# Sliding-window attention with a gated feed-forward on one core: values 0 and 1 moved ahead of scores 2 and 3, and pairs of units scored by chunks of 64 keys

## The chip, the core and the metric

The kernel runs on one core of a Trainium2 chip. Times are device microseconds (us) of that core for one execution. Engines are named as in the profile: PE (TensorE, matrix products), PEld (its weight loads), DVE (VectorE), ACT (ScalarE), POOL (GpSimd) and SP (SyncE, which only issues DMAs here).

## What is computed

Attention of 8 batches, 8 heads, 576 positions and head size 64, in which each position sees those at most 32 away, and then two matrix products with a sigmoid gate between them:

```python
scores = scale * np.matmul(q, k.transpose(0, 1, 3, 2))
mask = np.abs(pos[:, None] - pos[None, :]) <= 32
attn = softmax(np.where(mask, scores, -1e9))
x = np.matmul(attn, v).transpose(0, 2, 1, 3).reshape(4608, 512)
h = x @ w_in                               # 512 x 2048
out = (h / (1 + np.exp(-1.702 * h))) @ w_out   # 2048 x 512
```

## The kernel before, in words

The 4608 rows of all batches are one long row of queries, shifted by 32, so that a block of 64 queries sees exactly two blocks of 64 keys. **A unit** is 128 queries (36 units, `NU`); **a tile** is four units, 512 rows (9 tiles, `NT`). Everything is issued by hand in one order (`tc.manual_schedule()`): each engine works through its own instructions in the order in which the program names them, and waits where a semaphore says so.

For a unit, `scores` (L274) writes into two PSUM banks, one for even and one for odd heads: for each of four head pairs and each parity three matmuls of 64x64 weights (the keys) over 64, 128 and 64 columns of queries. Keys 0 to 63 and the 64 keys of the next unit land on the lower 64 partitions, keys 64 to 127 on the upper. The parity picks the upper or lower 64 rows of the array. Two `Exp` activations on ACT (L290, 128x512 each) turn the two banks into p. `band` (L292) multiplies p by the mask on DVE, in place. `values` (L300) multiplies p with v on PE, 16 matmuls of 65 columns; the 65th column of v is 1 and gives the sum. Half of them take v itself (`ve`), half a copy shifted by 64 rows (`vo`), which POOL makes (`odd_v`, L213). `norm` (L318) divides on DVE: one reciprocal and one product where both halves stand in tag `t`, two of each where they stand in two single banks. `x_T` transposes x for the first product: on PE with a copy by the engine named, or by a DMA.

The feed-forward runs on PE between these. `layer1_plain` and `layer2_plain` are ordinary products; `l1_group` and `layer2` compute a 2x2 block product with 7 instead of 8 products, whose sums (`w1_sums`, `w2_sums`, `x_sums`, `g_sums`) are made on DVE.

PSUM has eight banks under tags: `t` (two banks) and the single banks `A`, `B`, `C`, `E`, `LA`, `LB`. A tag is free when its last reader is done. Tiles in SBUF come from rings: `p` had four buffers of one unit, `qT` seven of one unit.

The opening (L600 to L723) loads parts of k and q, then v 0 to 3 and part of v 4, then w_in in pieces of 256, 256, 512 and more columns. All these are DMAs on POOL's one queue; each issue waits for the landing of the eighth before it. In the opening there is no band for units 0 to 3: `seed` puts the mask as a bias into the banks ahead of the scores, one 128x512 matmul a bank. The order on PE before is: transposes of k, seed 0, transposes of q, seed 1, scores 0, scores 1, transposes of the rest of k and q, seeds 2 and 3, scores 2 and 3, values 0 and 1, transposes of x 0 and 1, values 2 and 3, the first product of w_in (`l1(0, 0)`), transposes of x 2 and 3, then products. They end with the k transposes of the next tile (L677, `T_four`), from where both kernels have the same order except in `scores`.

Later places that the change touches: scores 4 and 5 in the opening (L694, L695), scores 8 and 9 in `run` (L840, L841), and `front` (L755, L756, L762, L763), which scores four units ahead of each of the tiles 3 to 7. In `run`, `band(8)` and `band(9)` follow on DVE at once, and behind them are sums, norm 8, band 10 and norm 9.

Of the kernel before, what the change touches and what calls it, by code (L numbers as in the profile page):

```python
# [16 lines left out]
BF16 = mybir.dt.bfloat16  # L17
# [9 lines left out]
class _Kernel:  # L27
# [7 lines left out]
    def __init__(self, ctx, tc, q, k, v, w_in, w_out, out):  # L35
        self.tc, self.nc = tc, tc.nc
        self.q, self.k, self.v, self.w_in, self.w_out, self.out = q, k, v, w_in, w_out, out
        self.B, self.H, self.S, self.D = q.shape
        self.N = self.B * self.S
        self.DM = self.H * self.D  # L40
        self.DFF = w_in.shape[1]
        self.scale = 1.0 / (self.D ** 0.5)
        self.NU = self.N // 128
        self.NT = self.N // TILE

        def pool(name, bufs, **kw):
# [7 lines left out]
        self.g, self.gs, self.o, self.sc = {}, {}, {}, {}  # L54

# [99 lines left out]
    def kq_tile(self, t):  # L155

        if ("T", t) not in self.stage:
            s = self.sb("gs", [128, 4, 576 + TILE], BF16, 2, "kq4")
            k, q = self.stage["T", t] = s[:, :, 0:576], s[:, :, 576:]
            for i in range(4):  # L160
                self.kT[4 * t + i] = k[:, :, 128 * i:128 * i + 128]
                self.qT[4 * t + i] = q[:, :, 128 * i:128 * i + 128]
            self.kT[4 * t + 4] = k[:, :, 512:576]
        return self.stage["T", t]

    def T_first(self, c, part, tags, engs):
# [95 lines left out]
    def score_banks(self, tag):  # L262
        if tag == "t":
            sc = self.bank(tag, name="sc")
            return [sc[:, 0], sc[:, 1]]
        return [self.bank(x, name="sc") for x in tag]

    def seed(self, u, tag):

        self.sc[u] = self.score_banks(tag)  # L270
        for x in self.sc[u]:
            self.mm(x, self.ident, self.bias, start=True)

    def scores(self, u, tag=None):  # L274
        kT, q = self.kT[u], self.qT[u]
        nxt = self.k_first if u == self.NU - 1 else self.kT[u + 1][:, :, 0:64]
        bias = tag is None
        sc = self.sc.pop(u) if bias else self.score_banks(tag)
        for hp in range(4):
            c = 128 * hp  # L280
            start = hp == 0 and not bias
            for eo in range(2):
                r = slice(64 * eo, 64 * eo + 64)
                lo, hi = sc[eo][0:64], sc[eo][64:128]
                self.mm(lo[:, c:c + 64], kT[r, hp, 0:64], q[r, hp, 0:64], start=start)
                self.mm(hi[:, c:c + 128], kT[r, hp, 64:128], q[r, hp, :], start=start)
                self.mm(lo[:, c + 64:c + 128], nxt[r, hp, :], q[r, hp, 64:128], start=False)
        p = self.p[u] = self.sb("p", [128, 2, 8, SQ], BF16, 4)
        for eo in range(2):
            self.nc.scalar.activation(p[:, eo].rearrange("k h s -> k (h s)"), sc[eo], AF.Exp, scale=self.scale)  # L290

    def band(self, u, eng=None):  # L292
        p = self.p[u]
        cross = [(2 * u + i) % 9 == 8 for i in range(2)]
        a, b = 0 if cross[0] else 1, 2 if cross[1] else 3
        pv = p.rearrange("p e (h b) s -> p (e h) b s", b=2)
        msk = self.mask[:, a:b + 1:b - a, :].rearrange("p (o b) s -> p o b s", o=1)
        (eng or self.nc.vector).tensor_mul(pv, pv, msk.to_broadcast([128, 8, 2, SQ]))  # L298

    def values(self, u, tag):  # L300
# [10 lines left out]
        for h in range(self.H):  # L311
            o = slice((h % 4) * (D + 1), (h % 4 + 1) * (D + 1))
            for blk in range(2):
                vt = (self.ve[u % 9], self.vo[u % 5])[blk]
                self.mm(acc[h // 4][64 * blk:64 * blk + 64, o], p[:, h % 2, h // 2 * 2 + blk, :], vt[:, h, :D + 1],
                        start=(h % 4 == 0))

    def norm(self, u):  # L318
# [281 lines left out]
    def opening(self):  # L600
# [57 lines left out]
        def l1(half, *fs, **kw):  # L658
            for f in fs:
# [1 line left out]
                n[0] += 1  # L661

        l1(0, 0)
        self.x_T(2, "B", act)
        self.x_T(3, "E", dve)
        l1(0, 2)
        l1(1, 0, 2)
        dve.tensor_copy(self.k_first, self.kT[0][:, :, 0:64])
        dve.tensor_copy(self.v_first, self.ve[0][0:64])
        l1(0, 4, 6)  # L670
        l1(1, 4, 6)
        for i in (3, 1, 2, 4):
            self.w1_sums((i,), 0)
# [17 lines left out]
        for u in (8, 9, 10, 11):  # L691
            self.fetch(u)
        h[:], n[0] = ["LB", "LA"], 0
        self.scores(4, "AC")  # L694
        self.scores(5, "t")  # L695
        l1(None, 12, later=gelus, kept=kept[2])
        self.scores(6, "BE")
        self.band(4)
# [40 lines left out]
    def front(self, t, late):  # L739
# [12 lines left out]
            return  # L752
        self.l2eng = self.nc.vector
        u = 4 * t + 4
        self.scores(u, "t")  # L755
        self.scores(u + 1, "AC")  # L756
        do(late, 2)
        do(l2, 20)
        do(late)
        xs = self.x_sums(t)  # L760
        do(xs, 1)
        self.scores(u + 2, "BE")  # L762
        self.scores(u + 3, "t")  # L763
        do(l2, 12)
        do(xs)

# [63 lines left out]
    def run(self):  # L830
# [130 lines left out]
```

## Time and profile before

| | |
|---|---|
| median of 3 runs | 282.11 us (281.75 to 282.63) |
| the profiled execution | 282.34 us |
| its span, first to last instruction | 280.5 us |
| mean granted PE clock | 0.993 |
| busy: PE, PEld, DVE, ACT, POOL | 268.9, 222.7, 212.1, 195.5, 133.1 us |
| moved by DMA | 37.61 MB |

The profile is of one execution. Its times count from the first instruction; about 1.8 us of the execution lie outside the span. A row of a timeline is: start, length, engine, line of the program, operation, what it writes and reads, shape, count, and in brackets the idle time of the engine before it and what ended it. A row of the chain is: start, length, what the end of the program was waiting for in that stretch. Busy time of PE includes the time that a matmul's last columns take to come through the array, so back-to-back matmuls overlap in it.

### The profile page before, as it was taken

How to read it: one execution, taken by the hardware profiler on the slowest of the kernel's cores; microseconds unless marked ns; L12 is line 12 of the kernel's file. 1: busy time of each engine (PE TensorE's matmuls, PEld its weight loads, DVE VectorE, ACT ScalarE, POOL GpSimd, SP SyncE). 2: the span in 40 equal slices, each digit the busy share in tenths (PEclk: the TensorE clock that was granted, in tenths of full speed). 3: DMA queues.
4: the chain of work that ended last, by engine and by line, in shares of the span. 5: the costliest groups of instructions: out<-in, count | busy, mean ns of one | idle time of the engine just before them, and what ended most of it. 6: DMA issues, size and time to landing. Idle time of an engine off the chain costs nothing.

```text
span 280.5 us, 8889 instructions
## 1 busy us (share of the span) xinstructions
PE 268.9 (96%) x3648; PEld 222.7 (79%) x3648; DVE 212.1 (76%) x492; ACT 195.5 (70%) x343; POOL 133.1 (47%) x199
## 2 busy tenths in 40 slices
PE   1979999999999999999999999999999999999995
PEld 1558756776888888888888888888888888888884
DVE  4454698897987798788888797888788887945731
ACT  2576893889897689658875887687759775567411
POOL 8895695999498248745694619441210000000000
PEclk9979999999999999999999999999999999999999
DMA  8999999999999999999999999999922051201033
GB/s 87 167 204 198 179 207 164 192 135 148 116 162 149 185 157 169 127 219 119 193 150 201 136 166 96 215 146 150 166 56 84 2 115 21 75 2 75 2 112 116
DMA packets 150265, 37.61 MB, mean 134 GB/s; under 512 B 138064, under 2 KB 145872, under 8 KB 150224
## 3 DMA queue, kind: packets, MB, share of 16 engines
q0 software_dynamic: 106656, 18.42, 95.0%
q1 hardware_dynamic: 43120, 18.10, 36.5%
q8 instruction: 28, 0.46, 0.7%
q10 hardware_dynamic: 448, 0.52, 0.6%
q14 instruction: 13, 0.11, 0.1%
HBM read 36.83 MB, written 9.44 MB: 165 GB/s over the span
## 4 chain that ended last, share of the span: by engine, by line
PE 93%; DVE 2%; ACT 2%; issue 1%; POOL 1%; ACTq 0%; POOLq 0%; DVEq 0%
PE o L70 40%; PE h L70 40%; PE sc L70 5%; PE pv L70 5%; PE tp L177 1%; PE tp L244 1%; ACT kq L67 1%; POOL kq L152 1%; PE tp L344 1%; DVE x L328 1%; PE tp L356 0%; ACT L680 0%; PE tp L201 0%; DVE kq L67 0%; DVE mask L111 0%
## 5 line engine op out<-in xcount | busy, mean ns | idle before, releaser
L459 ACT ACTIVATE g<-h 128x512 f16<-128x512 f32 x128 | 72.2, 598 | 35.1 <-PE h L70 34.9
L222 POOL COPY vo<-ve 64x264 int32<-64x264 int32 x71 | 32.9, 463 | 63.6 <-PE pv L70 41.3
L70 PEld LDWEIGHTS <-g 128*128 128x128 f16 x576 | 54.5, 98 | 10.1
L70 PE MATMUL h<-xs,a 128*128 128x256 f16 x384 | 57.6, 272 | 0.0
L70 PEld LDWEIGHTS <-a 128*128 128x128 f16 x512 | 49.5, 98 | 9.3 <-DVE xs L388 0.2
L70 PE MATMUL o<-w,g 128*128 128x256 f16 (+1 forms) x320 | 55.0, 294 | 0.0
L70 PE MATMUL h<-xT,w 128*128 128x256 f16 (+1 forms) x368 | 54.4, 281 | 0.0
L70 PEld LDWEIGHTS <-w 128*128 128x128 f16 x496 | 48.0, 98 | 7.7
L70 PEld LDWEIGHTS <-gs 128*128 128x128 f16 x384 | 36.7, 98 | 4.9 <-issue 0.2
L290 ACT ACTIVATE p<-sc 128x512 bf16<-128x512 f32 x72 | 36.9, 616 | 3.1 <-PE sc L70 2.9
L70 PE MATMUL o<-b,g 128*128 128x256 f16 x256 | 38.3, 273 | 0.0
L70 PE MATMUL o<-b,gs 128*128 128x256 f16 x256 | 37.7, 273 | 0.0
L472 DVE TENSOR_TENSOR h<-h,s 128x512 f32<-128x512 f32 x32 | 22.3, 698 | 19.2 <-PE h L70 19.0
L211 POOL DMA_DIRECT2D ve<-in_v_dram x40 | 34.3, 864 | 5.2 <-DMA w<-in_moe_w_out_dram 2.1
L67 ACT COPY h<-h 128x512 f32<-128x512 f32 x32 | 18.8, 588 | 16.7 <-PE h L70 16.3
L328 DVE TENSOR_TENSOR x<-pv,rec 128x256 f16<-128x256 f32 (+1 forms) x52 | 27.4, 527 | 1.8
L141 POOL DMA_DIRECT2D qst<-in_q_dram x35 | 28.1, 809 | 0.3
L141 POOL DMA_DIRECT2D kst<-in_k_dram x31 | 26.5, 856 | 1.3 <-DMA w<-in_moe_w_out_dram 1.3
L478 DVE TENSOR_TENSOR h<-h,s 128x512 f32<-128x512 f32 x32 | 22.4, 699 | 6.2 <-PE h L70 5.9
L298 DVE TENSOR_TENSOR p<-p,mask 128x1024 bf16<-128x1024 bf16 x32 | 22.3, 698 | 0.1
L67 ACT COPY s<-h 128x512 f32<-128x512 f32 x32 | 19.2, 600 | 1.2
L70 PE MATMUL h<-xs,w 128*128 128x256 f16 x128 | 19.2, 273 | 0.0
(87 smaller groups left out, 340.6 us busy)
## 6 DMA issues: line engine op xcount, KB each, us to landing
out_dram<-o_sb SPq DMA_DIRECT2D x33, 256.0 KB, 4.1
ve<-in_v_dram POOLq DMA_DIRECT2D x32, 128.0 KB, 6.6
kst<-in_k_dram POOLq DMA_DIRECT2D x25, 128.0 KB, 6.3
qst<-in_q_dram POOLq DMA_DIRECT2D x21, 128.0 KB, 5.8
w<-in_moe_w_out_dram POOLq DMA_DIRECT2D x4, 512.0 KB, 11.2
w<-in_moe_w_in_dram POOLq DMA_DIRECT2D x3, 512.0 KB, 9.6
qst<-in_q_dram POOLq DMA_DIRECT2D x7, 96.0 KB, 4.6
kq<-in_q_dram POOLq DMA_DIRECT2D x2, 256.0 KB, 5.9
```

The lines of the kernel that those rows point to most:

```text
L67: (eng.copy if eng is self.nc.scalar else eng.tensor_copy)(out, in_)
L70: self.nc.tensor.matmul(out, lhsT, rhs, start=start, stop=stop, skip_group_check=True)
L141: self.nc.gpsimd.dma_start(t[off:off + n], src[b, :, s:s + n, :].rearrange("h s d -> s h d"))
L152: self.nc.gpsimd.dma_start(self.stage["first"][0:n // j, :, at:at + j], src[0, :, lo:lo + n, :].rearrange("h (p j) d -> p h j d", j=j))
L211: self.nc.gpsimd.dma_start(t[off:off + n, :, :self.D], self.v[b, :, s:s + n, :].rearrange("h s d -> s h d"))
L222: eng.tensor_copy(*((words(vo[64:128]), words(self.ve[u % 9][64:128])), (words(vo[0:64]), words(nxt)))[i])
L290: self.nc.scalar.activation(p[:, eo].rearrange("k h s -> k (h s)"), sc[eo], AF.Exp, scale=self.scale)
L298: (eng or self.nc.vector).tensor_mul(pv, pv, msk.to_broadcast([128, 8, 2, SQ]))
L328: dve.tensor_mul(x[:, 4 * at:4 * (at + n), :].rearrange("p (b h) d -> p b h d", b=n), acc[:, :, :, :D], r.to_broadcast([128, n, 4, D]))
L459: act.activation(g[:, f, 256 * half:256 * half + 256], bank.rearrange("p (i n) -> p i n", i=2), AF.Gelu_apprx_sigmoid)
L472: dve.tensor_add(e, b, s7)
L478: dve.tensor_add(c, b, s7)
```

## The change

- `scores_pair` scores two units at once. The 256 queries of a pair lie side by side in one tile (`qTT`, three buffers), and the keys are taken in five chunks of 64 which see 64, 128, 128, 128 and 64 queries. This makes 40 matmuls for what were 48, over the same 4096 columns. Bank order changes: the first two banks hold head pairs 0 and 1 of both units, the last two head pairs 2 and 3. It is used for units 0, 2, 4, 8 and in `front` for 4t+4 and 4t+6; units 6, 7 and 10 to 15 keep `scores`.
- The p of two units is one tile (two buffers in place of four). An `Exp` covers two head pairs of both units. Each unit's p is then eight runs of 128 elements, 256 apart.
- In the opening, values 0 and norm 0 stand ahead of seeds 2 and 3 and their scores; the second half of pair 2's exps (`late=True`) comes behind the copy of x 0 on ACT; `l1(0, 0)` stands ahead of values 2 and 3; the banks of several steps change.
- `load_w1(0, 256)` is issued ahead of `load_v(3)`.

```diff
@@ place
+        if c == "q":
+            if u % 2 == 0:
+                two = self.qTT[u] = self.sb("qTT", [128, 4, 256], BF16, 3)
+                for i in range(2):
+                    self.qT[u + i] = two[:, :, 128 * i:128 * i + 128]
+            return self.qT[u]
@@ seed
-        self.sc[u] = self.score_banks(tag)
-        for x in self.sc[u]:
+        for x in self.score_banks(tag):
+            self.sc.setdefault(u, []).append(x)
             self.mm(x, self.ident, self.bias, start=True)
@@ scores
-        p = self.p[u] = self.sb("p", [128, 2, 8, SQ], BF16, 4)
+        if u % 2 == 0:
+            self.pp = self.sb("p", [128, 2, 2, 8, SQ], BF16, 2)
+        p = self.p[u] = self.pp[:, u % 2]
@@ new
+    def scores_pair(self, u, tags=None, late=False):
+        k = [self.kT[u], self.kT[u + 1], self.k_first if u + 2 == self.NU else self.kT[u + 2]]
+        q = self.qTT.pop(u)
+        sc = [x for tag in tags for x in self.score_banks(tag)] if tags else self.sc.pop(u)
+        for hp in range(4):
+            c, start = 256 * (hp % 2), hp % 2 == 0 and tags is not None
+            for eo in range(2):
+                r = slice(64 * eo, 64 * eo + 64)
+                bank = sc[2 * (hp // 2) + eo]
+                for i in range(5):
+                    lo, hi = max(0, 64 * (i - 1)), min(256, 64 * (i + 1))
+                    rows = slice(64 * (i % 2), 64 * (i % 2) + 64)
+                    self.mm(bank[rows, c + lo:c + hi], k[i // 2][r, hp, rows], q[r, hp, lo:hi], start=start and i < 2)
+        p = self.sb("p", [128, 2, 2, 2, 4, SQ], BF16, 2)
+        for i in range(2):
+            self.p[u + i] = p[:, :, :, :, 2 * i:2 * i + 2, :]
+        def exps(x):
+            for eo in range(2):
+                self.nc.scalar.activation(p[:, eo, x].rearrange("k h b s -> k (h b s)"), sc[2 * x + eo], AF.Exp,
+                                          scale=self.scale)
+        exps(0)
+        if not late:
+            exps(1)
+        return lambda: exps(1)
@@ opening
-        for u in (0, 1, 2, 3):
+        for u in (0, 1, 2):
             self.load_v(u)
+        self.load_w1(0, 256)
+        self.load_v(3)
         self.load_v(4, slice(0, 1))
-        self.load_w1(0, 256)
...
-        self.seed(1, "AC")
-        self.scores(0)
-        self.scores(1)
+        self.seed(0, "AC")
+        self.scores_pair(0)
         self.T_first("k", 1, ("LA", "LB"), (dve, dve))
         self.T_first("q", 1, ("B", "E"), (dve, act))
-        self.seed(2, ("LA", "LB"))
-        self.seed(3, "AC")
-        self.scores(2)
-        self.scores(3)
         self.values(0, "t")
         self.norm(0)
-        self.values(1, ("B", "E"))
+        self.seed(2, ("LA", "LB"))
+        self.seed(2, ("B", "E"))
+        exps = self.scores_pair(2, late=True)
+        self.values(1, "AC")
         self.norm(1)
-        self.x_T(0, "LA", act)
-        self.x_T(1, "LB", act)
-        self.values(2, "t")
-        self.norm(2)
-        self.values(3, "AC")
-        self.norm(3)
-        h, n = ["LA", "LB", "A", "C", "B", "E"], [0]
+        self.x_T(0, "t", act)
+        exps()
+        self.x_T(1, "A", dve)
+        h, n = ["LA", "LB", "C", "A", "B", "E"], [0]
...
         l1(0, 0)
-        self.x_T(2, "B", act)
-        self.x_T(3, "E", dve)
+        self.values(2, "t")
+        self.norm(2)
+        self.values(3, "BE")
+        self.norm(3)
         l1(0, 2)
+        self.x_T(2, "t", act)
+        self.x_T(3, "B", dve)
+        l1(0, 4, 6)
         l1(1, 0, 2)
...
-        l1(0, 4, 6)
@@ opening, run and front: each two calls of scores(u, ..), scores(u + 1, ..) become one, as here
-        self.scores(8, "t")
-        self.scores(9, "AC")
+        self.scores_pair(8, ("t", "AC"))
```

More of the change, by code (lines that the diff above doesn't have):

```diff
@@ L163, in kq_tile @@
             self.kT[4 * t + 4] = k[:, :, 512:576]
+            for i in (0, 2):
+                self.qTT[4 * t + i] = q[:, :, 128 * i:128 * i + 256]
         return self.stage["T", t]
@@ L256, in seed, with scores @@
     def seed(self, u, tag):
-        self.sc[u] = self.score_banks(tag)
-        for x in self.sc[u]:
+        for x in self.score_banks(tag):
+            self.sc.setdefault(u, []).append(x)
             self.mm(x, self.ident, self.bias, start=True)
[L262 to L274, printed above, removed]
+    def scores(self, u, tag):
         kT, q = self.kT[u], self.qT[u]
         nxt = self.k_first if u == self.NU - 1 else self.kT[u + 1][:, :, 0:64]
-        bias = tag is None
-        sc = self.sc.pop(u) if bias else self.score_banks(tag)
+        sc = self.score_banks(tag)
         for hp in range(4):
             c = 128 * hp
-            start = hp == 0 and not bias
+            start = hp == 0
             for eo in range(2):
@@ L295, in band @@
         a, b = 0 if cross[0] else 1, 2 if cross[1] else 3
-        pv = p.rearrange("p e (h b) s -> p (e h) b s", b=2)
+        pv = (p.rearrange("p e (h b) s -> p (e h) b s", b=2) if len(p.shape) == 4 else
+              p.rearrange("p e y z b s -> p (e y z) b s"))
         msk = self.mask[:, a:b + 1:b - a, :].rearrange("p (o b) s -> p o b s", o=1)
@@ L314, in values @@
                 vt = (self.ve[u % 9], self.vo[u % 5])[blk]
[L315 removed]
+                w = p[:, h % 2, h // 2 * 2 + blk, :] if len(p.shape) == 4 else p[:, h % 2, h // 4, h // 2 % 2, blk, :]
+                self.mm(acc[h // 4][64 * blk:64 * blk + 64, o], w, vt[:, h, :D + 1],
                         start=(h % 4 == 0))
@@ L693, in opening @@
         h[:], n[0] = ["LB", "LA"], 0
-        self.scores(4, "AC")
-        self.scores(5, "t")
+        self.scores_pair(4, ("AC", "t"))
         l1(None, 12, later=gelus, kept=kept[2])
@@ L754, in front @@
         u = 4 * t + 4
-        self.scores(u, "t")
-        self.scores(u + 1, "AC")
+        self.scores_pair(u, ("t", "AC"))
         do(late, 2)
@@ L761, in front @@
         do(xs, 1)
-        self.scores(u + 2, "BE")
-        self.scores(u + 3, "t")
+        self.scores_pair(u + 2, ("BE", "t"))
         do(l2, 12)
```

2 lines of the change are left out of this document (1 added, 1 removed).

## The prediction

> **What bounds the kernel now.** I read the page first (span, clock line, chain by engine), then the chain and the timelines of the opening, then each place where the new pairs stand.
>
> ```profile
> span 280.5 us, 8889 instructions
> ...
> PE 93%; DVE 2%; ACT 2%; issue 1%; POOL 1%; ACTq 0%; POOLq 0%; DVEq 0%
> ```
>
> TensorE carries 93% of the chain that ended last, and from about 21 us on it hardly waits. So the change can win in two ways: fill the holes of the first 21 us, or make the score matmuls shorter. It loses wherever a new wait reaches TensorE. The page's clock line dips in the opening; three windows show it:
>
> ```profile
> 10.26:13.67 3.41, 3.07 (x103) 2.09 (x106) 1.89 (x3) 2.54 (x5) 2.56 (x6) 1.00 2.40 155
> 13.67:17.08 3.41, 2.05 (x87) 1.44 (x77) 1.93 (x6) 2.65 (x5) 3.15 (x7) 1.00 1.44 200
> 17.08:20.49 3.41, 3.24 (x45) 2.48 (x45) 1.93 (x6) 1.97 (x3) 3.41 (x5) 0.50 1.24 207
> ```
>
> The columns are window, length, busy us of PE, PEld, DVE, ACT and POOL, then the granted clock (1.00, 1.00, then 0.50) and the DMA. After a window with PE busy for 2.05 of 3.41 us the clock was halved for 3.4 us. The chain there:
>
> ```profile
> 16.20 0.43 DVE x L328
> ...
> 16.91 0.34 issue
> ...
> 17.51 1.02 PE pv L70 x16
> 18.53 1.82 PE h L70 x8
> 20.35 0.58 PE tp L344 x8
> 20.93 6.99 PE h L70 x64
> 27.91 1.06 PE tp L201 x32
> ```
>
> TensorE waits for VectorE's norm of unit 1, transposes, runs values 2 and 3, then at half clock the first 8 products with w_in (1.82 us; 64 of them at full clock take 6.99, so 8 take 0.87). The k transposes of the next tile (27.91) are my finish line for the opening: what stands in between is the same work in both kernels.
>
> **Part 1, the opening.** The rows that set the new order:
>
> ```profile
> 10.80 2.07 ACT L290 ACTIVATE p<-sc 128x512 bf16<-128x512 f32 x4 [0.70 <-PE sc L70]
> 12.73 1.33 POOL L222 COPY vo<-ve 64x264 int32<-64x264 int32 x3 [0.51 <-DVE kq L67]
> 12.74 0.81 PE L70 MATMUL sc<-bias,ident 128*128 128x512 bf16 x3 [0.22 <-DVE kq L67]
> 14.59 0.21 DVE L327 RECIPROCAL rec<-pv 128x8 f32<-128x8 f32 x1 [1.31 <-PE pv L70]
> 15.44 0.17 DVE L327 RECIPROCAL rec<-pv 128x4 f32<-128x4 f32 x1
> ```
>
> Values 0 now stand right behind the transposes of q. They need the four exps of pair 0 (10.80 + 2.07 = 12.87) and the first shifted copy of v, GpSimd's first of three from 12.73 (done about 13.14). So they start at 13.2; before, the norm's reciprocal of their result stood at 14.59, so they ran some 0.9 later. The four seeds of units 2 and 3 queue behind them, and behind those the pair's scores. Values take about 0.25 a unit, the four seeds 0.2 each, the pair's scores 0.5, each change of shape about 0.1; values 1 start near 15.1 and end at 15.4.
>
> VectorE gets norm 0 at 13.7, long before it matters, and norm 1 at 15.5. Norm 1 took from 15.44 to 16.63 before, so it ends near 16.65 now: later by the scores of the second pair that went ahead. What is late next is this norm; the transpose of x 1 ends near 17.0, its copy (0.42 on VectorE) near 17.5, and the first w_in product starts near 17.6 instead of 18.53. ScalarE runs exps(0), the copy of x 0, then the late exps: 15.0 + 1.0 + 0.5 + 1.1 = 17.6, before values 2 ask for them. Values 2 follow at 18.5, values 3 to 19.0, a product to 20.0, x 2 to 20.2. Norm 3 follows norm 2 on VectorE and ends near 21.0, so the transpose of x 3 ends at 21.2. Seven groups of 8 products are then left, 56 x 0.109 = 6.1: the k transposes start near 27.47 against 27.91. **Gain 0.44 us**, if the clock stays full from 13 us on.
>
> The w_in columns. Before, values 3, the rest of values 4 and both quarter loads of w_in were the DMAs that stood between values 2 and the 512-column load; they are exchanged, no byte is added. The first product doesn't start before 17.6 by the norms above, and the first quarter would have landed by 16.9 where it stood (issued at 9.30, 7.6 to landing):
>
> ```profile
> 9.30 2.41 POOL L125 DMA_DIRECT2D w<-in_moe_w_in_dram  x3
> w<-in_moe_w_in_dram POOLq DMA_DIRECT2D x1, 256.0 KB, 7.6
> 16.64 0.89 POOL L190 DMA_DIRECT2D o_sb<-in_k_dram  x1
> o_sb<-in_k_dram POOLq DMA_DIRECT2D x1, 512.0 KB, 9.3
> ```
>
> So it gains nothing. It makes GpSimd's copies of values 3 wait longer by one quarter load (256 KB at the window's 200 GB/s, 1.3 us), and what is queued behind them is the issue of the next k and q loads (16.64, now about 17.4). The k load takes 9.3 us to landing because it queues behind loads of w_in, so I cost this at nothing too; without that cover it is 0.8 us on a load that TensorE needs at 27.9.
>
> Ends for the opening: at best the half clock cost and the 0.34 issue gap are both gone and the norms overlap better, -0.9; at worst the half clock strikes a denser stretch, +0.6.
>
> **Part 2, 40 matmuls for 48.** Fourteen pairs: 0, 2, 4, 8, and 16 to 34. Columns streamed are the same.
>
> ```profile
> 128.75 0.70 PE L70 MATMUL sc<-qT,kT 64*64 64x64 bf16 x48
> 69.63 0.38 PE sc L70 x16
> 128.82 0.63 PE sc L70 x32
> L70 PE MATMUL sc<-qT,kT 64*64 64x128 bf16 x2 | 0.2, 240 | 0.0
> L70 PE MATMUL sc<-qT,kT 64*64 64x64 bf16 x2 | 0.2, 213 | 0.0
> ```
>
> The second and third rows are of the chain (some matmuls are merged there): one unit costs 0.38, two cost 0.63, so a further unit is 0.25. A unit puts eight 64-column matmuls on each of the two tiles of the array that hold keys 0 to 63; 0.25/8 = 31 ns each. The other two tiles have four of 128 columns, about 55 ns each by the 0.109 of a 256-column one. The last two rows are the first 35 ns of a batch: two of each shape have started, though the program's order is 64, 128, 64, 64, 128, 64. The second 128 passed the third 64, so the tiles run side by side and the fullest tile sets the time. In a pair it has 64, 128, 64 for each of four head pairs: 4 x (31 + 55 + 31) = 0.47, against 16 x 31 = 0.50. **0.03 us a pair.** Ends: 0, and eight matmuls at 0.63/48 = 13 ns, 0.10 us, if issue is what bounds. I take 0.02, nearest to the tiles' row, as the first pair of each front also waits for its bank C to come free: ten pairs in the fronts give **-0.2 us** (0 to -1.0).
>
> **Part 3, bands wait for four exps instead of two.** Each exp now covers two head pairs of both units, so band u needs the whole pair. In the steady fronts the bands run 2 us after the exps and feel nothing. At unit 8 they follow at once:
>
> ```profile
> 68.68 2.06 ACT L290 ACTIVATE p<-sc 128x512 bf16<-128x512 f32 x4
> 69.84 1.63 DVE L298 TENSOR_TENSOR p<-p,mask 128x1024 bf16<-128x1024 bf16 x2
> 71.39 0.42 DVE L402 TENSOR_TENSOR gs<-gs,g 128x512 f16<-128x512 f16 x1
> ...
> 74.51 0.42 DVE L328 TENSOR_TENSOR x<-pv,rec 128x256 f16<-128x256 f32 x1
> 74.99 0.22 PE L70 MATMUL pv<-ve,p 128*64 128x65 bf16 x1
> ```
>
> Band 8 began at 69.84, after two exps; now after four, at 68.68 + 2.06 = 70.74 and the 0.03 of a wake-up. Band 9 waited for the same fourth exp, and the g sum came 0.61 behind its start (71.39 - 70.78); with both bands behind that exp the g sum starts at 72.0, **0.61 late**, and the timeline shows no idle time of VectorE from there to 77 us that could make it good. Queued behind band 8 are band 9, two g sums, norm 8, band 10 and norm 9. Values 10 wait for norm 9 already: their second half started at 74.99, right after 74.51 + 0.42 = 74.93. So TensorE is held by nearly the whole delay: **+0.6 us** (0.4 to 0.6). At unit 4 the same, smaller:
>
> ```profile
> 33.54 4.05 ACT L290 ACTIVATE p<-sc 128x512 bf16<-128x512 f32 x8 [0.57 <-PE sc L70]
> 35.34 0.69 DVE L298 TENSOR_TENSOR p<-p,mask 128x1024 bf16<-128x1024 bf16 x1
> ...
> 38.12 0.68 DVE L298 TENSOR_TENSOR p<-p,mask 128x1024 bf16<-128x1024 bf16 x1
> 38.86 0.22 PE L70 MATMUL pv<-ve,p 128*64 128x65 bf16 x1
> ```
>
> The fourth exp ends at 33.54 + 2.07 = 35.61; band 4 moves from 35.34 to 35.64, and with what is queued behind it on VectorE (a copy, band 5, norm 4; a short idle time there gives 0.12 back) band 6 from 38.12 to 38.30, and values 6, which started 0.06 after band 6 ended, by **+0.18**. The band over a strided p keeps the same runs of 128 elements; I leave it at 0.69, and a dearer one would show first at unit 8. The transposed q written into half of a pair's tile and the two p tiles per pair have covers of tens of us.
>
> **Sum.** -0.44 - 0.2 + 0.6 + 0.18 = +0.15 us. The profiled execution took 282.34 us (span 280.5 and 1.8 around it), 0.23 above the median of 282.11. 282.34 + 0.15 = **282.5**: no change that a measurement tells.
>
> **Rivals.** (a) *The clock is halved again.* In the new order TensorE still waits from about 15.7 to 17.5, with short transposes between; windows of 3.41 us there hold, by the terms of part 1 and the 0.2 us that a lone matmul's busy time outlasts its stream, 2.3 us of busy PE (an estimate), a little over the 2.05 after which the clock was halved, well under the 3.07 of the window ahead of it, which kept it. If it strikes, the denser stretch pays: 8 products 0.9 us more, values 0.3, less what the norms cover, about 0.9: 283.4, slower. It decides from the point where 2.3 us of 3.41 count as too little. The Trainium skill ("TensorE: Matmul & The Clock Gate", Part 1) says that the clock falls after an idle window of some 3.4 us whose phase runs free. This trace agrees on the length (3.41 us at 0.50), while its window was 60% busy; by that page's idleness neither order would be throttled.
>
> (b) *Matmuls start strictly in order.* Then in a pair each head pair's second parity waits until the first's fifth matmul has started, 31 + 55 = 86 ns, twice per head pair: 4 x 172 = 0.69 us against 0.50, +0.19 for each pair, and 12 pairs on the path make +2.3, and the fronts' 0.2 is not won: 285.0. The Trainium skill (the same page, Part 3, what overlaps) has matmuls start in program order and only weight loads pulled ahead; the rows of the first 35 ns above speak against that here.
>
> (c) *Issue bounds the scores:* -0.10 a pair, 281.6. For it: 13 ns each fits 0.63/48; against it: 0.38 for 24 doesn't halve. (d) *The bands' delay is absorbed:* 281.7; against it stands the back-to-back VectorE from 69.84 to 77.
>
> **Chances.** Forecast 0.42, (a) 0.30, (b) 0.06, (c) 0.10, (d) 0.07, others 0.05. Within 0.3% (0.85 us, about what a measurement of this kernel tells from no change) are 0.33 of the forecast, 0.07 of (a), 0.06 of (c), 0.04 of (d): 0.50 in all. Slower are 0.08 of the forecast, 0.23 of (a), all of (b) and 0.02 of the others: 0.39. The rest, 0.11, is faster. The range takes in the forecast with its bounds, (a), (c) and (d), and leaves out (b): 281.2 to 284.0.
>
> **What would show it.** Right: the first w_in product near 17.6, the k transposes near 27.5; a pair of scores at 0.60 in the chain; band 8 starting at the end of the fourth exp and a hole of TensorE in values 10. Wrong: a clock of 0.50 between 17 and 22 us (then a); pairs at 0.5 (c) or 0.8 (b); no hole at unit 10 (d).

## The result, and the profile after

The changed kernel takes 283.93 us in the median of 21 runs (283.13 to 286.16), the kernel before 282.71 in 21 runs beside them. The ratio is 1.0049, with a 95% interval of 1.0032 to 1.0065: slower by about 1.4 us. The forecast was no change that a measurement tells (282.5); 283.93 lies inside its range of 281.2 to 284.0, but other terms make it up. The profiled execution of after took 283.94, so it is a typical one. Its page:

```profile
span 282.2 us, 8654 instructions
...
PEclk9999999999999999999999999999999999999999
...
PE 82%; ACT 5%; DMA 5%; DVE 4%; POOL 2%; issue 1%; POOLq 0%; DVEq 0%
```

No dip of the clock; but DMA, absent from the chain before, now holds 5% of it, and TensorE lost 11 points. The chain of after in the opening (start, length, what):

```profile
17.52 1.03 PE h L70 x8
18.55 0.39 PE pv L70 x16
...
21.06 0.28 PE tp L371 x2
21.34 6.11 PE h L70 x56
27.46 1.06 PE tp L203 x32
```

The first w_in product starts at 17.52 (forecast 17.6), the k transposes at 27.46 (forecast 27.47; 27.91 before). Unit 4 and unit 8 in the same chain:

```profile
33.08 2.07 ACT p L309 x4
35.16 0.02 issue
35.18 0.69 DVE p L324
...
68.95 1.58 ACT p L309 x3
70.53 0.02 issue
70.56 1.29 DVE p L324 x2
71.85 0.35 DVE gs L429
...
74.95 0.43 DVE x L355
75.39 0.04 issue
75.43 0.32 PE pv L70 x8
75.75 0.38 PE sc L70 x16
```

The bands start at the end of the fourth exp, both times, and at unit 8 VectorE then runs without a pause until values 10 get their bank. The scores of unit 13 start 0.44 after those of before (75.31), although TensorE was 0.25 ahead at 68.6. That was forecast; what follows was not:

```profile
100.07 0.51 issue
100.59 6.73 DMA xT<-x
107.32 0.03 issue
107.35 0.02 DVEq L415
107.37 0.04 issue
107.41 0.42 DVE xs L415
...
109.04 1.05 PE h L70 x8
```

Tile 3's sums of x wait for the DMA that transposes unit 15's x: issued at 100.59, landed at 107.32. TensorE loses 0.9 there. Another loss stands behind the last matmul. The rows of SyncE's last instructions (line of the kernel's end, engine's queue, operation, count: shortest, median, longest ns, first and last start), after and before:

```profile
L979 SPq DRAIN  x3: 7/7/122, 281.2 to 281.6; - x3
```

```profile
L956 SPq DRAIN  x3: 7/7/7, 279.7 to 280.0; - x3
```

The first drain comes 0.6 after the last store landed (280.60) instead of 0.27 (279.42), and takes 122 ns.

To see where each execution loses or gains, the start of the same matmul was compared in all traces. The table gives it in us against the first profiled execution of before; minus is earlier. Its places: first transpose of the next tile's k; the last matmuls of values 6; a layer 2 product ahead of unit 8's bands; values 11; a layer 2 product ahead of tile 3; a product behind the start of tile 5; the last tile. The k column is the first transpose's own start; the chain above counts its stretch 0.07 later. The last column is the time from the last matmul's end to the end of the span.

| trace | k (27.85) | values 6 (38.86) | 68.60 | values 11 (77.04) | 101.74 | 164.63 | 259.72 | end |
|---|---|---|---|---|---|---|---|---|
| before | 0 | 0 | 0 | 0 | 0 | 0 | 0 | 3.38 |
| before, again (e13) | -0.70 | -0.70 | -0.71 | -0.71 | -0.71 | -0.34 | -0.33 | 3.46 |
| after | -0.46 | -0.22 | -0.25 | +0.44 | +0.41 | +1.45 | +1.40 | 3.82 |
| after, again (e9) | -0.20 | +0.16 | +0.26 | +0.95 | +1.09 | +1.02 | +0.97 | 3.74 |
| e1 | -0.42 | -0.07 | -0.07 | -0.07 | -0.02 | -0.06 | -0.11 | 3.73 |
| e2 | -0.54 | -0.54 | -0.53 | -0.53 | -0.57 | -0.43 | -0.48 | 3.81 |
| e4 | -0.60 | -0.36 | -0.39 | +0.30 | +0.27 | +0.11 | +0.05 | 3.94 |
| e6 | -0.67 | -0.44 | -0.47 | +0.22 | +0.18 | +0.66 | +0.67 | 3.42 |
| e7 | -0.34 | +0.10 | +0.21 | +0.21 | +0.17 | +2.08 | +2.03 | 3.79 |
| e16 | -0.52 | -0.52 | -0.54 | -0.54 | -0.55 | +2.46 | +2.53 | 3.41 |

One more difference lies behind the last place. Before's chain has VectorE idle for 0.40 ahead of a copy in the last tile, for which no view names a reason:

```profile
275.25 0.40 issue
275.65 0.44 DVE o_sb L558
```

TensorE waits for that copy. The copy is VectorE's instruction 575 in the trace (its first has number 0), and the same delay of 0.40 to 0.41 stands ahead of number 575 in e13 and e4, where it is the same copy, and in e5, where it is the copy before. In the other 16 traces another instruction has that number, and TensorE's last eight products stand 0.21 earlier against before than the products ahead of them. So after's last matmul ends only 1.19 later than before's, not 1.40.

### The profile page after: what moved, and what is told of

The parts are those of the page before. It is cut to its first block, busy times and chain, and to the rows that moved or that the text cites. A ratio compares the mean times of both kernels' runs of the same rounds, so it can differ in the third digit from the quotient of the medians.

```text
span 282.2 us, 8654 instructions
## 1 busy us (share of the span) xinstructions
PE 269.3 (95%) x3536; PEld 221.9 (79%) x3536; DVE 212.9 (75%) x493; ACT 194.9 (69%) x342; POOL 132.3 (47%) x199
## 4 chain that ended last, share of the span: by engine, by line
PE 82%; ACT 5%; DMA 5%; DVE 4%; POOL 2%; issue 1%; POOLq 0%; DVEq 0%
PE h L70 37%; PE o L70 37%; PE pv L70 4%; PE sc L70 3%; DMA xT<-x 2%; DMA ve<-in_v_dram 2%; ACT p L309 2%; DVE p L324 1%; DVE x L355 1%; POOL kq L152 1%; PE tp L252 1%; ACT kq L67 1%; ACT g L486 1%; PE tp L383 0%; ACT L309 0%
## 5 line engine op out<-in xcount | busy, mean ns | idle before, releaser
L224 POOL COPY vo<-ve 64x264 int32<-64x264 int32 x71 | 32.1, 452 | 67.2 <-PE pv L70 44.8
L70 PE MATMUL h<-xT,w 128*128 128x256 f16 (+1 forms) x368 | 53.7, 277 | 0.6 <-ACT p L309 0.6
L309 ACT ACTIVATE p<-sc 128x512 bf16<-128x512 f32 x56 | 28.5, 621 | 2.9 <-PE sc L70 2.8
```

The costliest lines, as they stand in the source:

```text
L70: self.nc.tensor.matmul(out, lhsT, rhs, start=start, stop=stop, skip_group_check=True)
L224: eng.tensor_copy(*((words(vo[64:128]), words(self.ve[u % 9][64:128])), (words(vo[0:64]), words(nxt)))[i])
L309: self.nc.scalar.activation(p[:, eo, x].rearrange("k h b s -> k (h b s)"), sc[2 * x + eo], AF.Exp, scale=self.scale)
```

## The experiments

Theory at the start: beside the forecast's own steps (opening, bands) there is a stall at tile 3 of 0.9. Rival: that stall is only the lateness of unit 8 handed on.

**e1, units 8 and 9 single** (the rest as changed).

```diff
-        self.scores_pair(8, ("t", "AC"))
+        self.scores(8, "t")
+        self.scores(9, "AC")
```

> Units 8 and 9 are scored singly again, the rest is the changed kernel. Both theories: the hole of TensorE at values 10 goes, scores of unit 13 start near 74.65 in the profile (75.75 in the changed kernel, 75.31 before). Theory (the transposes of x for tile 3 are late because of the DMA and SyncE side, the q transposes into halves of a pair's tile among it): the stall ahead of tile 3's first sums stays at about 0.9 us, the last x transpose still lands near 107, and the time is 0.66 under the changed kernel: 283.3, +0.2% against before. Rival (that stall is only the lateness of unit 8 handed on): it goes too, the last x transpose lands near 106, and the time is 1.5 to 1.7 under the changed kernel: 282.3, -0.15% against before.

Measured: 283.12, ratio 1.0018 (0.9986 to 1.0050). In the table the lag stays at -0.07 from values 6 to values 11: unit 8's whole 0.69 is gone. (The 74.65 expected for unit 13 took that price off twice; it started 0.51 before after's.) No stall at tile 3 either, which spoke for the rival, until e9.

**e2, units 4 and 8 single:** as e1, and `scores(4, "AC")`, `scores(5, "t")` for the pair at 4.

> Units 4 and 5, 8 and 9 are scored singly; the new opening and the pairs of the fronts stay. Theory: the 0.45 of the opening is kept whole up to tile 2 (transposes of x 4 near 41.2, scores of unit 13 near 74.85), then tile 3's stall of about 0.9 us takes it back: 283.1, +0.15% against before. Rival (the stall is the lateness of units 4 and 8 handed on): 282.2, -0.2% against before. The prediction's 0.02 us for each pair in the fronts is in either number as 0 to 0.2.

Measured: 282.05, 0.9987 (0.9953 to 1.0021). The lag is -0.54 from the opening to tile 3: nothing is lost at units 4 and 8. Its fronts, with pairs, give 0.02 to 0.03 each.

**e3, pairs in the opening alone:** e2, and the fronts with four single calls of `scores`.

> Pairs stand only in the opening (units 0 to 3); all others are scored singly, but q's transposes still go into halves of a pair's tile. Theory: within 0.2 us of the kernel with single units 4 and 8 alone, so about 283.1, with tile 3's stall still there, and a pair in the fronts is worth 0 to 0.02 us. Rival 1 (the pairs in the fronts bring the stall or cost time on their banks): 282.2, -0.2% against before, and no stall at tile 3. Rival 2 (pairs in the fronts gain what the prediction's bound allows, 0.1 each): 1.0 us over the kernel with units 4 and 8 single.

Measured: 284.59, 1.0048 (1.0015 to 1.0081). Neither theory gives that. Its profiled execution (283.06, one of the fastest) shows one stall, 0.9 at tile 5, again the sums of x behind a DMA. What the other executions do is taken up in e14, e16 and e18.

**e4, the old opening,** whole, with its order of loads; all later pairs kept.

```diff
-        self.scores_pair(0)
...
-        exps = self.scores_pair(2, late=True)
...
+        self.scores(0)
+        self.scores(1)
...
+        self.scores(2)
+        self.scores(3)
...
```

> The opening up to the transposes of the next tile is that of before; all later pairs (4, 8 and the fronts) stay. Theory: nothing of the opening is gained, units 4 and 8 cost 0.2 and 0.66, tile 3's stall 0.9: 284.4, +0.6% against before, transposes of k at 27.9 and scores of unit 13 near 76.2. Rival (the stall at tile 3 comes from the new opening's order of loads, so that all later DMAs are shifted): no stall, 283.5, +0.3% against before.

Measured: 283.33, 1.0015 (0.9982 to 1.0049). The surprise is its k transposes, 0.60 *ahead* of before's with before's own order: both openings are as fast here. Unit 4 cost 0.20 and unit 8 0.69 again.

**e5, transposes of x ahead of those of q 19 and k 20** in SyncE's queue.

```diff
-            if (t, n) != (3, 0):
+            if (t, n) not in ((2, 3), (3, 0)):
                 self.turn(u + n + 4)
...
             self.l1_group(t, n, fill, side)
+            if (t, n) == (2, 3):
+                self.turn(u + n + 4)
```

> The changed kernel, with the transposes of q 19 and k 20 issued behind those of x 14 and x 15 on SyncE instead of ahead of them (tile 3's boundary alone). Theory (the stall ahead of tile 3's sums is the last x transpose, which stands behind two more transposes in SyncE's queue): x 15's transpose is issued right behind its norm, near 99.3 instead of 100.59, and lands 1 us earlier; VectorE waits under 0.2 us for it, TensorE's 0.9 us of stall are gone, and the time is 0.9 under the changed kernel: 283.0, +0.1% against before. Rival (the DMA engines are full there, whatever the order of the queue): it still lands near 107, the stall stays, 283.9.

Measured: 286.18, 1.0152 (1.0105 to 1.0199). The wait for x is gone, and k's transpose is late in its place. Waits from 100 to 112 us (engine, line, for what: total, times, longest):

```profile
PEld L70 <- DMA kT<-kst: 2.7, 1, 2.7
PE sc L70 <- DMA kT<-kst: 2.6, 1, 2.6
```

In after SyncE issues six transposes back to back from 92.7 to 101.8 there, 1.3 us each and more, and TensorE asks for k's and VectorE for the last of x's within a few us. This exchange doesn't mend the order.

**e6, more instructions on SyncE:** the four stores of tile 0 cut into three by rows.

```diff
+            for lo, hi in ((0, 48), (48, 96), (96, n)) if t == 0 else ((0, n),):
+                self.nc.sync.dma_start(self.out[row + lo:row + hi, :], o[lo:hi, i, :])
```

> The changed kernel, with the four output stores of tile 0 (at 50 to 58 us, SyncE idle) cut into three by rows each, so that SyncE has 8 instructions more before the end. Theory (SyncE takes 0.37 us more ahead of its instruction with the number 207 of the trace, which in the changed kernel is the last drain and in the kernel before is a wait for a store that has not landed yet): the place moves 8 instructions ahead, behind a wait, and the span ends 3.3 us after the last matmul instead of 3.75: 0.43 under the changed kernel, 283.5. Rival (the longer end is of the last stores or of the changed program as such): the end stays at 3.75 and the time at 283.9. The same run is a second look at tile 3: theory on it, a stall of 0.9 again; rival (chance of one execution): another size.

Measured: the end is 3.42, as before, and its drains are short again:

```profile
L980 SPq DRAIN  x3: 7/7/7, 280.2 to 280.5; - x3
```

In the trace 0.34 to 0.36 us pass ahead of SyncE's instruction 207 (its first has number 0) in every one of the 19 traces that have so many. In before it is a wait for a store that lands later anyway; in after, with five instructions fewer, it is the first drain; here it comes at 276.2 us, ahead of a store that waits for its data until 277.2. The Trainium skill ("Runtime: NRT & Kernel Launch", Instruction fetch mechanics) says that an engine's instructions are fetched in blocks of 256 and that crossing a block is mostly hidden. The place at a fixed count agrees, if some 49 instructions that the trace doesn't list come first; hidden it is in before and here, and not in after. That it is a fetch is not shown: in before (279.00 to 279.34) and here (275.88 to 276.23) the DMA records have no packet of an instruction queue in that time. The median came to 283.91, 1.0056 (1.0034 to 1.0078), no better than after: the end is mended and something else varies more. Its stall at tile 3 was 0.1.

**e7, two g sums ahead of bands 8 and 9.**

```diff
         do(more, 12)
+        do(late)
         self.band(8)
         self.band(9)
-        do(late)
```

> The changed kernel, with the two last g sums of tile 1 ahead of bands 8 and 9 on VectorE instead of behind them. Theory (unit 8's price is VectorE's time behind the fourth exp: it idles 0.88 us ahead of band 8 and has two sums of 0.45 us behind it): the sums fill the idle time, norms 8 and 9 come 0.9 earlier, the hole of TensorE at values 10 is gone, scores of unit 13 start near 75.0 instead of 75.75, 0.66 under the changed kernel: 283.3. Rival (the price is the exps or the pair's matmuls themselves): scores of unit 13 stay near 75.75, 283.9.

Measured: 283.00, 1.0028 (1.0006 to 1.0050). The lag stays at +0.21 over unit 8. The bands' rows of the timeline, in e9 (the changed kernel) and here; the bracket is VectorE's idle time ahead of them:

```profile
71.06 1.29 DVE L324 TENSOR_TENSOR p<-p,mask 128x1024 bf16<-128x1024 bf16 x2 [0.88 <-ACT p L309]
```

```profile
71.01 1.29 DVE L324 TENSOR_TENSOR p<-p,mask 128x1024 bf16<-128x1024 bf16 x2
```

The pair is still there, its bands still wait for four exps, and it costs nothing: unit 8's price was VectorE's idle 0.88 us with 0.9 us of sums queued behind it. The rival (exps or matmuls of the pair) is out.

**e8, mended:** e2 with the edits of e5, e6 and e7.

> The new opening and the pairs of the fronts, units 4 and 8 scored singly, the g sums ahead of bands 8 and 9, x 14 and 15 ahead of q 19 and k 20 in SyncE's queue, and SyncE's 8 instructions more. Theory: against the kernel before, the opening's 0.45 to 0.55 is kept, no lag at units 4 and 8, no stall at tile 3, no longer end: 282.0 against 282.7 before, -0.25%, faster than both kernels. Rival (x transposes at later tiles are late by chance and take the gain): within 0.1% of before.

Measured: 286.69, 1.0125 (1.0076 to 1.0174). Up to tile 3 it is 0.58 ahead, and its end is 3.27; but e5's wait for k is in it, and at tile 3 it falls back by 4.3. The chain there, where 12 products of layer 2 take 1.42 in e5:

```profile
100.36 5.81 DMA kT<-kst
106.17 0.04 issue
106.21 0.66 PE sc L70 x25
106.87 2.67 PE o L70 x12
```

```profile
103.40:106.80 3.40, 1.12 (x42) 0.76 (x40) 2.02 (x6) 1.43 (x4) 0.24 (x1) 1.00 1.70 236
106.80:110.20 3.40, 3.40 (x20) 2.42 (x18) 1.40 (x4) 1.87 (x4) 3.29 (x6) 0.50 1.21 153
```

So some 1.2 of it is the half clock that followed the wait, behind a window with PE busy for 1.12 us: a long stall is paid for once more.

**e9, the changed kernel again,** not a letter changed.

> The changed kernel once more, for a second trace of the same program. Theory (the size of the stall at the boundaries of tiles 3 to 5 is the luck of one execution: the last transpose of x takes 5.5 to 9.6 us to land and VectorE's sums ask for it after 6): the lag of TensorE against before ahead of tile 3 is near +0.4 again and the end behind the last matmul is 3.75 again, but the stalls at tiles 3 to 5 have other sizes than 0.9, 0.1 and 0. Rival (the 0.9 at tile 3 belongs to the program): 0.9 at tile 3 again, within 0.2. Time 283.9, 1.2 over before, in both.

Measured: 283.13, 1.0038 (1.0018 to 1.0058). No stall at tiles 3 to 5 in this execution (+1.09 to +1.02 in the table, with 0.15 of before's own at tile 5). So the 0.9 was not the program's. Unit 8 costs 0.69 again, unit 4 0.13, the opening is only 0.20 ahead.

**e10, last transposes of x of tiles 3 to 5 on TensorE.**

```diff
-                        self.x_T(u + n)
...
+        do(l2, 8)
+        if t < 6:
+            self.x_T(u - 1, "B", self.nc.vector)
+        do(l2, 12)
```

> The changed kernel, with the last transpose of x of tiles 3, 4 and 5 (units 15, 19, 23) made by TensorE, and copied by VectorE, instead of by DMA. Costs some 0.25 to 0.3 of TensorE each, 0.8 in all. Theory (those transposes' landing makes both the stalls and the spread between executions): no wait for them at tiles 3 to 5 in the trace, the middle half of the executions lies within 0.4 us of each other (1.0 in the changed kernel), median 283.9 - 1.2 + 0.8 = 283.5. Rival (the spread and the stalls come from elsewhere): the spread stays and the median rises by the whole 0.8, 284.7.

Measured: 283.23, 1.0040 (1.0024 to 1.0055), against e9's 283.13 on the same chip: the 0.8 of added work costs 0.1. The middle half of its executions spans 0.6 us, of e9's 0.9, the slowest is 283.93 against 284.43. That speaks for the theory, though less than expected, and 12 runs a side are few for a spread.

**e11, mended without the exchange:** e8 without e5's edit.

> The new opening and the pairs of the fronts; units 4 and 8 scored singly; the g sums ahead of bands 8 and 9; SyncE's 8 instructions more; the order of SyncE's queue at tile 3 as in the changed kernel. Theory: TensorE 0.55 ahead of before from the opening to the end, ahead by 0.6 with the fronts' pairs, the end behind the last matmul 3.3 again: 0.6 under before, -0.2%, if the x transposes are no later than before. Rival (they are late by chance more often, as TensorE asks for them earlier): same as before, within 0.1%.

Measured: 282.64, 1.0004 (0.9976 to 1.0031). 0.6 ahead up to tile 3, end 3.41; then stalls of 0.4 at tile 3 and 0.8 at tile 5 in the profiled execution take it back.

**e12, e11 with e10's edit.**

> The kernel with units 4 and 8 single, sums ahead and SyncE's longer program, and the last transpose of x of tiles 3, 4 and 5 by TensorE. Theory: 0.8 of TensorE more, no wait for those transposes, so the narrowest spread of all; time 0.2 over before in the fastest executions, equal or under it in the median. Rival (the DMA transposes weren't the spread): 0.8 over the same kernel with DMA transposes.

Measured: 283.35, 1.0034 (1.0015 to 1.0052). The middle half spans 0.4 us, of e11's 1.2. But e2's spans 0.4 to 0.5 too, with every one of these transposes by DMA, so the spread alone doesn't show that they make it. The profiled execution of e12 was its slowest; there k's transpose was 1.1 late at tile 4.

By then the opening was open: was it the new order that was fast, or the one execution of before that was slow?

**e13, the kernel before again,** unchanged.

> The kernel before, once more. Theory (its first profiled execution had the clock halved from 17 to 20.5 us, by chance): in an execution at full clock the first product with w_in starts near 18.2 instead of 18.53 and the k transposes near 27.25 instead of 27.91, no later than in the changed kernel (27.46); executions with a mean clock of 0.994 or less are 0.8 us slower than the others and are a quarter to a third of all. Rival (the new order gains 0.45 whatever the clock): 27.9 again at full clock.

Measured: 282.24 against 282.90 for the same program run beside it, ratio 0.9968 (0.9939 to 0.9997): a reminder of what such an interval is worth. Its chain and its windows (busy us of PE, PEld, DVE, ACT, POOL, granted clock, DMA):

```profile
17.45 0.40 PE pv L70 x16
...
19.94 0.29 PE tp L344 x2
20.23 6.99 PE h L70 x64
27.22 1.06 PE tp L201 x32
```

```profile
13.67:17.08 3.41, 2.23 (x88) 1.62 (x88) 1.93 (x6) 2.65 (x5) 3.10 (x8) 1.00 1.45 199
17.08:20.49 3.41, 3.07 (x54) 2.31 (x54) 2.14 (x7) 2.94 (x4) 3.41 (x5) 1.00 1.24 206
```

At full clock the old order has its k transposes at 27.22, 0.24 ahead of after's.

**e14, the opening alone, end mended:** e3 with e6's edit.

> Only the opening is new (units 4, 8 and the fronts scored singly; q still transposed into pair tiles), and SyncE has 8 instructions more, so that the end isn't longer. Theory: nothing against executions of before at full clock, 0.8 less than those at half clock, 0.2 less on the mean: -0.1% to 0 against before. Rival (the prediction's gain): -0.45, -0.16% against all of before and -0.6 against its executions at half clock.

Measured: 285.11, 1.0058 (1.0026 to 1.0090), like e3 and against both theories; the profiled execution (282.71) was the fastest of its runs.

**e15, pairs in the fronts alone:** old opening, units 4 and 8 single, e6's edit.

> Only the fronts' units are scored in pairs (the old opening, units 4 and 8 single), with SyncE's longer program. Theory: 0.02 to 0.03 us less of TensorE in each of the fronts 3 to 7, 0.1 in all, which no median shows: 0 against before, with half-clock executions as often as in the kernel before. Rival (prediction's term): -0.2 to -1.0.

Measured: 282.20, 0.9963 (0.9936 to 0.9989), and 0.9968 for the kernel before itself (e13) on that chip: no difference that this shows. Its profiled execution was struck by the clock too, one us later than before's. The windows here are laid to the moments at which its own clock changed:

```profile
14.72:18.14 3.42, 2.17 (x66) 1.43 (x59) 2.14 (x8) 2.81 (x7) 3.20 (x7) 1.00 1.35 203
18.14:21.55 3.41, 3.40 (x21) 2.67 (x21) 2.35 (x8) 2.33 (x3) 3.41 (x6) 0.50 1.25 207
```

**e16 and e18, the program of e14 in two more executions.**

> The kernel with only the opening new and SyncE's longer program, looked at again. Theory (the last x transposes of tiles 3 to 5 land late in the typical execution): an execution of 284 us or more shows waits of 1 to 3 us for them and nothing else new ahead of 100 us. Rival (the opening itself takes longer in the typical execution): k transposes later than 27.8.

> The same kernel as in the look ahead of this one, once more, with the same theory and rival: a wait for x transposes at tiles 3 to 5, or a longer opening.

Measured: 284.66 and 283.60. Both openings are fast (-0.52, -0.46), and the loss is where the theory put it: 0.3 at tile 3 and 2.7 at tile 5 in e16, 0.3, 1.0 and 0.4 at tiles 3, 4 and 5 in e18. VectorE's wait at tile 5 in e16, for a transpose that took 9.2 us to land:

```profile
DVE xs L415 <- DMA xT<-x: 2.4, 1, 2.4
```

**e17, q's transposes into tiles of one unit,** else e14.

```diff
-        if c == "q":
-            if u % 2 == 0:
-                two = self.qTT[u] = self.sb("qTT", [128, 4, 256], BF16, 3)
...
```

> The opening new, all later units scored singly, and q's transposes into tiles of one unit as in the kernel before; SyncE's 8 instructions more stay. Theory (the excess comes with q's pair tiles, whose DMAs wait for two units' scores): back to before, 0 to -0.1%. Rival (it comes with the opening, or with the output stores cut in three): +0.5%, 284.3 to 285.

Measured: 285.01, 1.0107 (1.0069 to 1.0145). The excess stays (1.8 from tile 3 to behind tile 5 in the profiled execution), so q's pair tiles are not its cause.

## Why the prediction was wrong, step by step

**Part 1, the opening: the step that failed.** The new order came out at the forecast, 27.46 for 27.47. That it did so to 0.01 us is luck: the terms shown add to 27.3 (21.2 + 6.1), and the traces of the new order lie between 27.1 and 27.8. What failed is what it was set against: "then at half clock the first 8 products with w_in", taken as a property of the kernel before. It was the lot of this execution, not of each. At full clock the old order reaches the k transposes 0.70 (e13) and 0.60 (e4) ahead of that execution; the 16 traces of the new order reach them 0.05 to 0.71 ahead, 0.49 in the mean. So against an execution of before at full clock the opening is worth not -0.44 but about +0.15 (0.65 less 0.49; the 0.65 is of two traces), and the forecast counted a gain that most runs of before don't leave to be had. The 0.95 us that the half clock adds to 8 products (1.82 - 0.87) is more than the whole gain forecast; that alone was reason to ask what the old order does without it.

How often does it strike? Executions whose mean clock is 0.994 or less (1.00 in e13, 0.994 in e15, 0.993 in before) are 44 of 158 with the old opening, and 1 of 147 with the new one (e5 and e8, with their 3 us waits elsewhere, left out). On the chip of e9 to e12 the 12 such runs of before have a median of 282.7, the other 20 of 281.9. In the other sets of runs of before the same two medians lie 0.3, 0.9, 1.0 and 2.2 apart, so the price is known roughly, and the mean clock doesn't say where in a run the dip was. The new opening does remove the half clock, worth some 0.8 in about 3 runs of 10; rival (a), which let it strike the new order with a chance of 0.30, had it the wrong way round.

What decides whether it strikes can be read in part, if the windows of 3.41 us are counted from the moment at which the trace's record of the clock first has it full. This moment differs: 10.26 in before, 10.49 in e13, 11.31 in e15, 12.12 in e4. In such windows the old opening has its emptiest one with PE busy for 2.05 us in before and 2.17 in e15, and half clock right behind both; 2.21 in e13 and 2.33 in e4, and full clock behind both:

```profile
13.90:17.31 3.41, 2.21 (x88) 1.51 (x84) 1.93 (x6) 2.65 (x5) 3.16 (x7) 1.00 1.42 201
17.31:20.73 3.42, 3.10 (x56) 2.51 (x56) 2.38 (x8) 2.94 (x4) 3.42 (x6) 1.00 1.24 206
```

The new opening's emptiest windows hold 2.23 to 2.51 in its 16 traces, near the 2.3 that rival (a) estimated, and full clock stands behind all of them. So in the openings of these 20 traces it is the place of the windows that decides, by a few hundredths of a us of busy time. It is no rule for the whole kernel: windows of 1.75 (e5), 1.94 (e16) and 2.00 (e7) at tiles 3 and 5 kept full clock too. The Trainium skill ("TensorE: Matmul & The Clock Gate", Part 1) calls the activity window free-running, with the number of slow matmuls varying from run to run; the four moments above agree. The prediction quoted the free phase and drew only the idleness from that section.

**Part 2, the pairs' matmuls: right, with about half of the gain.** A pair stands in after's chain as forecast:

```profile
130.24 0.60 PE sc L70 x30
```

Over the five fronts e2 gains 0.02, 0.02, 0.03, 0.03 and 0.02, together 0.12 where 0.2 was forecast. With 0.60 for a pair, and neither 0.8 nor 0.5, rivals (b) and (c) are out.

**Part 3, the bands: right.** Unit 8 cost 0.68 to 0.69 in all six traces that have it as changed (0.6 forecast; 0.25 + 0.44 in after), unit 4 0.13 to 0.20 (0.18 forecast), and in e1, e7 and e9 another 0.15 to 0.25 ahead of values 4. Unit 4's price is less sure than unit 8's: of the nine traces with the new opening and units 4 and 5 single, e3, e8, e17 and e18 lose 0.08 to 0.18 there too, the other five nothing. Rival (d), the delay absorbed, is out; e7 shows what it would have taken.

**What was costed at nothing.** "The transposed q written into half of a pair's tile and the two p tiles per pair have covers of tens of us": true as far as it goes, but with them the transposes' waits changed, SyncE's program got five instructions shorter (e17, without the pair's tiles, has five more than e14), and the end 0.45 longer (1.55 to 1.57 from the last landing to the end in the traces with instruction 207 at the drain, 1.10 to 1.12 in those of before and of e6). And no step looked at the deadline of SyncE's transposes at tiles 3 to 5, though before's own trace has VectorE wait 0.3 for one at tile 3. In the profiled execution of after it cost 0.9 more; e9 shows 0. It is a lottery that both kernels play, with 0 to 2.8 us lost at one tile in the traces with the new opening and up to 0.5 in those with the old.

**The sum, made again,** against executions of before at full clock: +0.15 opening, +0.2 unit 4, +0.69 unit 8, -0.12 fronts, +0.45 end, and -0.21 for VectorE's delay in the last tile, which before has and after hasn't: +1.16. (The forecast's own four terms add to +0.14.) Measured +1.4 (0.9 to 1.8) and, in e9, +1.1 (0.5 to 1.6); the runs of before contain 3 in 10 at half clock, which brings the means 0.2 closer, and the late transposes of both kernels come on top. The same terms give e1 +0.47 (measured +0.5), e7 +0.47 (+0.8), e11 -0.18 (+0.1), e2 +0.27 (-0.4, interval -1.3 to +0.6) and, without the -0.21, e4 +1.2 (+0.4, interval -0.5 to +1.4); e6's +0.7 lies under its interval (1.0 to 2.2). So the sum explains the size of the loss in after and e9, and not each variant.

**Left open:** why the kernels with the new opening and single units in the fronts (e3, e14, e17) take 1.4 to 3 us more than before, while e2 and e11 with pairs there do not. Between e2 and e3, on one chip, the pairs of the fronts alone make 2.5 in the medians, twenty times what their matmuls gain; with the old opening (e15) no such gain shows. Where the time goes is shown in four traces (late transposes of x in e3, e16, e17 and e18); what in the order of issue brings it is not, nor whether each slow execution has it.

No version here is shown to beat the kernel before: e15's interval lies under 1, but so does that of before against itself on that chip (e13), and e11, which has the faster end, the sums ahead and no lag, equals it.

## What to carry to other kernels

Before a dip of the clock is counted as something to win, look whether other executions have it: the mean clock of each run stands beside its time. When a dip is examined, count the windows from that execution's own change of clock. A new wait on an engine with work queued behind it cost 0.69 here (unit 8, 0.88 us of idle VectorE), and nothing once independent work was put into it (e7). Where a queue issues transposes back to back, look at who waits for each; moving x's ahead made k's late (e5).

## What the runs showed of the hardware

- 0.35 us ahead of SyncE's instruction 207, at the same count in 19 traces with five different programs on SyncE; 0.45 of the end when it falls on the first of the last drains.
- A DMA transpose of one unit's x, 128x512, takes 1.2 us of SyncE to issue and lands 2.8 (e6, tile 4) to 9.6 us (e7, tile 5) later as the last of its tile; in the same place of the same program, at tile 3, 6.73 (after) and 5.49 (e9).
- A granted clock of 0.50 for 3.41 us behind a window with PE busy for 2.05 (before) and 2.17 us (e15) of it, and none behind 2.21 (e13), with the windows counted from each execution's first full clock; at tiles 3 and 5 windows of 1.75 to 2.00 (e5, e16, e7) kept full clock. A mean clock of 0.994 or less in 44 of 158 executions of one order of work, and in 1 of 147 of another.
- 0.40 us ahead of VectorE's instruction 575, a copy in the last tile, in before, e13, e4 and e5; the other 16 traces are 0.21 better there.
